# Seven half-size products in place of eight for the first expert layer, with a running sum in one PSUM bank

## The chip, the cores and the metric

One core of one Trainium2 chip. The metric is the time of one execution on the device in microseconds (us), as a median over repeated runs. All runs below were in the fast state, with a granted TensorE clock (as a share of full speed) of 0.98 or more over the span.

## The reference, cut to what matters

An attention over sorted blocks makes x (3072 tokens by 512), and a dense mixture of eight experts follows. The experts take four fifths of the time, and only their first layer is changed:

```python
N, D, E, F = (3072, 512, 8, 1024)
...
for e in range(E):
    h = np.maximum(x @ w1[e], 0.0)      # first layer: contraction over D = 512
    ye = h @ w2[e]                      # second layer: contraction over F = 1024
    out += P[:, e:e + 1] * ye
```

## The kernel before

The tokens stand in six columns of 512. One block of the first layer (`h_block`) makes 128 hidden features of one column with four matmuls of 128x512 in bf16, and ScalarE clamps it out of PSUM, the memory that matmuls write to and add up in. The kernel uses it as a ring of eight banks, each of which holds one result of 128x512; a bank can be used again when its result has been read out (evicted). One tile of the second layer (`y_tile`) takes eight matmuls, and VectorE scales it and adds it to the fp32 result. The first 76 blocks (experts 0 and 1) are made earlier, between the attention's matmuls. Then the expert loop runs: four tiles of one column, then the next blocks, up to nine columns ahead.

```python
    def bank(shape, dt=F32):                       # a ring of 8 PSUM banks
        return ps.tile(shape, dt, name="bank")
    # ... cut ...
    def h_block(e, c, fb, both=False):
        if fb == 0:
            hT[e, c] = hp_.tile([128, 8, 512], BF16, name="hTs")
        b_ = bank([128, 512])
        for kk in range(4):
            nc.tensor.matmul(b_, w1t[e][:, kk, fb * 128:(fb + 1) * 128], xf[:, kk, c * 512:(c + 1) * 512],
                             start=(kk == 0), stop=(kk == 3))
        # ... cut: while attention runs, every other one goes to VectorE ...
            nc.scalar.activation(out=hT[e, c][:, fb, :], in_=b_, func=AF.Relu)
    # ... cut ...
    def y_tile(e, c, tt):
        t = c * 4 + tt
        b_ = bank([128, Dm])
        for fb in range(8):
            nc.tensor.matmul(b_, hT[e, c][:, fb, tt * 128:(tt + 1) * 128], w2t[e][:, fb, :],
                             start=(fb == 0), stop=(fb == 7))
        # ... cut: expert 0 only scales ...
            nc.vector.scalar_tensor_tensor(out=osbl[:, t, :], in0=b_, scalar=glog[:, t, e:e + 1],
                                           in1=osbl[:, t, :], op0=ALU.mult, op1=ALU.add)
    # ... cut ...
    for n, (e, c) in enumerate(seq):               # 48 columns of experts
        for tt in range(4):
            y_tile(e, c, tt)
        # ... cut: weight loads ...
        while state["h"] < len(blocks) and (state["h"] // 8) - n < HB - 1:
            fill(1, both=False)                    # one h_block
```

The softmax here doesn't subtract the row's maximum and nothing guards it: scores larger than these inputs give would overflow.

Of the kernel before, what the change touches and what calls it, by code (L numbers as in the profile page):

```python
# [11 lines left out]

F32 = mybir.dt.float32
BF16 = mybir.dt.bfloat16
AF = mybir.ActivationFunctionType
AX = mybir.AxisListType
ALU = mybir.AluOpType
ENG = mybir.EngineType

def mkap(t, dims, off=0):  # L20
    return bass.AP(tensor=t.tensor, offset=t.offset + off, ap=dims)

@with_exitstack
def kernel(
# [11 lines left out]
    nc = tc.nc  # L36
    B, H, S, D = 4, 8, 768, 64
    NB = 8
    NPAIR = 16
    N, Dm, E, F = 3072, 512, 8, 1024  # L40
    NT = 24
    HB = 10
    scale = 1.0 / (D ** 0.5)

    ones = ctx.enter_context(tc.tile_pool(name="ones", bufs=1))
    wp = ctx.enter_context(tc.tile_pool(name="wp", bufs=2))
    hp_ = ctx.enter_context(tc.tile_pool(name="hp", bufs=HB))
    ps = ctx.enter_context(tc.tile_pool(name="ps", bufs=8, space=bass.MemoryType.PSUM))

    def bank(shape, dt=F32):  # L50
        return ps.tile(shape, dt, name="bank")
# [18 lines left out]
    kh = k.rearrange("b h (p kk) d -> (b h) p kk d", kk=6)  # L70
    vh = v.rearrange("b h (p kk) d -> (b h) p kk d", kk=6)
    actx = ExitStack()
    iop = actx.enter_context(tc.tile_pool(name="iop", bufs=5))
    atp_ = actx.enter_context(tc.tile_pool(name="atp", bufs=2))
    qkv = {}
# [9 lines left out]
    w1t, w2t = {}, {}  # L85

    def load_w1(e):
        w1t[e] = wp.tile([128, 4, F], BF16, name="w1e")
        nc.gpsimd.dma_start(out=w1t[e], in_=moe_w1[e].rearrange("(kk k) f -> k kk f", k=128))  # L89

    def load_w2(e):
        w2t[e] = wp.tile([128, 8, Dm], BF16, name="w2e")
        nc.gpsimd.dma_start(out=w2t[e], in_=moe_w2[e].rearrange("(fb k) f -> k fb f", k=128))  # L93
# [6 lines left out]
    xtT = ones.tile([128, 4, B, 6, 128], BF16)  # L100
    xf = xtT.rearrange("d hp b kk p -> d hp (b kk p)")
    glog = ones.tile([128, NT, E], F32)

    order = tc.manual_schedule(engines={ENG.PE, ENG.Activation, ENG.DVE, ENG.Pool, ENG.SP})
    order.__enter__()
# [3 lines left out]
        nc.tensor.matmul(w_, wide[:, 0:128], wide, start=True, stop=True)  # L109

    rs = ones.tile([32, 8], F32)
    Prep = ones.tile([32, 8, 8, 16], BF16)
    Pt = P.rearrange("p i j -> p j i")
    nc.vector.reduce_max(out=rs, in_=P, axis=AX.X)
    nc.vector.tensor_sub(P, P, mkap(rs, [rs.ap[0], rs.ap[1], [0, 8]]))
    for it in range(5):
# [4 lines left out]
                                op=ALU.mult)  # L121
        nc.vector.reduce_sum(out=rs, in_=Pt, axis=AX.X)  # L122
        nc.vector.reciprocal(out=rs, in_=rs)
        if it < 4:
            nc.vector.tensor_tensor(out=Pt, in0=Pt, in1=mkap(rs, [rs.ap[0], rs.ap[1], [0, 8]]),
                                    op=ALU.mult)
        else:
            nc.vector.tensor_tensor(out=Prep, in0=mkap(P, [P.ap[0], [8, 8], [1, 8], [0, 16]]),  # L128
                                    in1=mkap(rs, [rs.ap[0], [0, 8], [1, 8], [0, 16]]), op=ALU.mult)
    pbp = bank([128, 8, 32])  # L130
    for i in range(8):
        nc.tensor.matmul(pbp[:, i, :], Prep[:, i].rearrange("g j c -> g (j c)"),
                         ident[0:32, 0:32], start=True, stop=True)
    Pbig = ones.tile([128, 8, 32], F32)
    nc.vector.tensor_copy(Pbig, pbp)

    KT, VT, QT, ATT, VS, OG = {}, {}, {}, {}, {}, {}

    vs_ = [ones.tile([96, 8, 2, 65], BF16, name=f"vs{n}") for n in range(2)]
    for t in vs_:  # L140
        nc.vector.memset(t[:, :, :, 64:65], 1.0)

# [87 lines left out]

    hT = {}
    flip = [0]

    def h_block(e, c, fb, both=False):
        if fb == 0:
            hT[e, c] = hp_.tile([128, 8, 512], BF16, name="hTs")
        b_ = bank([128, 512])
        for kk in range(4):
            nc.tensor.matmul(b_, w1t[e][:, kk, fb * 128:(fb + 1) * 128], xf[:, kk, c * 512:(c + 1) * 512],  # L239
                             start=(kk == 0), stop=(kk == 3))  # L240
        flip[0] ^= 1
        if both and flip[0]:
            nc.vector.tensor_scalar_max(hT[e, c][:, fb, :], b_, 0.0)  # L243
        else:
            nc.scalar.activation(out=hT[e, c][:, fb, :], in_=b_, func=AF.Relu)  # L245

    early = [(0, 0), (1, 0), (0, 1), (0, 2), (1, 1), (1, 2), (0, 3), (1, 3), (0, 4), (0, 5), (1, 4), (1, 5)]
    seq = early + [(e, c) for e in range(2, E) for c in range(6)]
    blocks = [(e, c, fb) for e, c in seq for fb in range(8)]
    last_batch = [0, 1, 1, 2, 3, 3]  # L250
    state = {"h": 0, "done": -1}

    def spin(n):
        b_ = bank([128, 512])
        for _ in range(n):
            nc.tensor.matmul(b_, wide[:, 0:128], wide, start=True, stop=True)  # L256

    def fill(n, both=True):
        for _ in range(n):
            if state["h"] >= len(blocks):  # L260
                return
            e, c, fb = blocks[state["h"]]
            if last_batch[c] > state["done"]:
                if state["done"] < 0:
                    spin(1)
                return
            h_block(e, c, fb, both)
            state["h"] += 1
# [33 lines left out]
    for it in range(8):  # L302
# [3 lines left out]
                                op=ALU.mult)  # L306
        nc.vector.reduce_sum(out=cs2, in_=glog.rearrange("p t e -> p e t"), axis=AX.X)
        fill(3, both=False)
        b_ = bank([128, E])
# [3 lines left out]
                                       in1=mkap(cs1, [cs1.ap[0], [0, NT], cs1.ap[1]]),  # L313
                                       op0=ALU.mult, op1=ALU.mult)
# [4 lines left out]
    osbl = mpc.tile([128, NT, Dm], F32)  # L319
# [3 lines left out]
# [6 lines that stand above are left out]
        if e == 0:  # L329
            nc.vector.tensor_scalar(out=osbl[:, t, :], in0=b_, scalar1=glog[:, t, e:e + 1],  # L330
                                    scalar2=None, op0=ALU.mult)
        else:
            nc.vector.scalar_tensor_tensor(out=osbl[:, t, :], in0=b_, scalar=glog[:, t, e:e + 1],  # L333
                                           in1=osbl[:, t, :], op0=ALU.mult, op1=ALU.add)
        if e == E - 1:
            bb, kk = divmod(t, 6)
            nc.sync.dma_start(out=out[bb * S:(bb + 1) * S].rearrange("(p kk) d -> kk p d", kk=6)[kk],
                              in_=osbl[:, t, :])

    left = {e: 6 for e in range(E)}  # L340
    hleft = {e: 6 for e in range(E)}
    for e, c, fb in blocks[:state["h"]]:
        if fb == 7:
            hleft[e] -= 1
    if hleft[0] == 0:
        load_w1(2)
    if hleft[1] == 0:
        load_w1(3)
    for n, (e, c) in enumerate(seq):
        for tt in range(4):  # L350
            y_tile(e, c, tt)
        left[e] -= 1
        if left[e] == 0 and e + 2 < E:
            load_w2(e + 2)
        while state["h"] < len(blocks) and (state["h"] // 8) - n < HB - 1:
            e1, _, fb1 = blocks[state["h"]]
            fill(1, both=False)
            if fb1 == 7:
                hleft[e1] -= 1
                if hleft[e1] == 0 and e1 + 2 < E:  # L360
                    load_w1(e1 + 2)
    order.__exit__(None, None, None)

_INS = ['q', 'k', 'v', 'sort_net', 'moe_w_gate', 'moe_w1', 'moe_w2']
# [25 lines left out]
```

## Time and profile before

| | before |
|---|---|
| time, median of 13 runs | 749.34 us (748.73 to 750.14) |
| span of the profiled execution | 748.3 us |
| TensorE busy | 98% |
| ScalarE / VectorE / GpSimd busy | 37% / 34% / 7% |

Matmuls overlap, so the TensorE row of "busy" says little about stalls; the distance from start to start does.

### The profile page before, as it was taken

How to read it: one execution, taken by the hardware profiler on the slowest of the kernel's cores; microseconds unless marked ns; L12 is line 12 of the kernel's file. 1: busy time of each engine (PE TensorE's matmuls, PEld its weight loads, DVE VectorE, ACT ScalarE, POOL GpSimd, SP SyncE). 2: the span in 40 equal slices, each digit the busy share in tenths (PEclk: the TensorE clock that was granted, in tenths of full speed). 3: DMA queues.
4: the chain of work that ended last, by engine and by line, in shares of the span. 5: the costliest groups of instructions: out<-in, count | busy, mean ns of one | idle time of the engine just before them, and what ended most of it. 6: DMA issues, size and time to landing. Idle time of an engine off the chain costs nothing.

```text
span 748.3 us, 10583 instructions
## 1 busy us (share of the span) xinstructions
PE 733.7 (98%) x4508; PEld 358.5 (48%) x4588; DVE 252.1 (34%) x497; ACT 274.2 (37%) x497; POOL 48.9 (7%) x71
## 2 busy tenths in 40 slices
PE   6999999999999999999999999999999999999997
PEld 3776665444444444444444444444444444444443
DVE  5887775632122122121221221221221221212443
ACT  2776665513423423324324324234234233243000
POOL 7542000000000000000000000000000000000000
PEclk8999999999999999999999999999999999999999
DMA  9999100011300062200330032100330003000133
GB/s 147 204 205 165 19 2 1 1 22 36 56 1 1 0 95 31 44 1 1 56 57 1 0 57 40 18 0 1 57 56 1 1 0 57 1 0 1 43 154 141
DMA packets 29679, 33.21 MB, mean 44 GB/s; under 512 B 1984, under 2 KB 22464, under 8 KB 29632
## 3 DMA queue, kind: packets, MB, share of 16 engines
q0 software_dynamic: 26128, 26.23, 22.4%
q1 hardware_dynamic: 3504, 6.30, 2.2%
q8 instruction: 36, 0.59, 0.3%
q14 instruction: 11, 0.09, 0.0%
HBM read 52.45 MB, written 6.29 MB: 79 GB/s over the span
## 4 chain that ended last, share of the span: by engine, by line
PE 97%; DVE 1%; issue 1%; ACT 0%; DMA 0%; ACTq 0%
PE bank L327 44%; PE bank L239 44%; PE bank L162 2%; PE bank L207 2%; PE bank L195 1%; PE bank L188 1%; PE bank L256 1%; PE bank L218 1%; PE bank L173 1%; PE bank L227 0%; DMA P<-in_sort_net_dram 0%; PE bank L310 0%; DVE rs L122 0%; ACT P L117 0%; DVE Prep L128 0%
## 5 line engine op out<-in xcount | busy, mean ns | idle before, releaser
L245 ACT ACTIVATE hTs<-bank 128x512 bf16<-128x512 f32 x358 | 213.7, 597 | 371.2 <-PE bank L239 363.1
L239 PE MATMUL bank<-xtT,w1e 128*128 128x512 bf16 x1490 | 341.9, 379 | 1.9
L327 PE MATMUL bank<-w2e,hTs 128*128 128x512 bf16 x1503 | 336.0, 379 | 1.7
L333 DVE SCALAR_TENSOR_TENSOR osbl<-bank,glog,osbl 128x512 f32<-128x512 f32 x168 | 126.1, 751 | 398.8 <-PE bank L327 386.0
L327 PEld LDWEIGHTS <-hTs 128*128 128x128 bf16 x1536 | 150.3, 98 | 181.0
L239 PEld LDWEIGHTS <-w1e 128*128 128x128 bf16 x1536 | 147.8, 98 | 170.3
L330 DVE TENSOR_SCALAR osbl<-bank,glog 128x512 f32<-128x512 f32 x24 | 18.0, 751 | 54.7 <-PE bank L327 51.7
L191 ACT ACTIVATE at<-bank 96x384 bf16<-96x384 f32 x64 | 26.0, 486 | 8.7 <-PE bank L188 8.4
L211 DVE TENSOR_TENSOR OG<-bank,rc 96x256 bf16<-96x256 f32 x64 | 26.9, 421 | 2.2
L89 POOL DMA_DIRECT2D w1e<-in_moe_w_dram x8 | 6.0, 754 | 312.6 <-PE bank L239 312.3
L93 POOL DMA_DIRECT2D w2e<-in_moe_w_dram x8 | 7.1, 890 | 237.5 <-PE bank L327 161.9
L243 DVE TENSOR_SCALAR hTs<-bank 128x512 bf16<-128x512 f32 x26 | 17.8, 683 | 6.1 <-PE bank L239 6.1
L220 ACT COPY xtT<-bank 128x768 bf16<-128x768 bf16 x16 | 12.8, 799 | 14.1 <-PE bank L218 13.7
L167 ACT CAST KT<-bank 128x384 bf16<-128x384 f32 x32 | 13.8, 485 | 8.1 <-PE bank L162 7.9
L207 PEld LDWEIGHTS <-at 96*96 96x96 bf16 x256 | 14.1, 125 | 2.8
L207 PE MATMUL bank<-vs,at 96*96 96x65 bf16 x256 | 13.9, 209 | 0.0
L81 POOL DMA_DIRECT2D kb<-in_k_dram x16 | 11.5, 718 | 18.5 <-PE bank L162 16.8
L169 DVE CAST VT<-bank 128x384 bf16<-128x384 f32 x16 | 8.9, 553 | 11.2 <-PE bank L162 8.8
L198 DVE COPY vs<-bank 96x1024 bf16<-96x1024 bf16 x16 | 11.0, 690 | 4.2 <-PE bank L195 3.8
L210 DVE RECIPROCAL rc<-bank 96x4 f32<-96x4 f32 x64 | 10.9, 170 | 3.7 <-PE bank L207 3.7
L81 POOL DMA_DIRECT2D vb<-in_v_dram x16 | 11.5, 717 | 7.4 <-PE bank L162 2.8
L81 POOL DMA_DIRECT2D qb<-in_q_dram x16 | 11.5, 717 | 2.1 <-PE bank L256 0.9
(57 smaller groups left out, 187.2 us busy)
## 6 DMA issues: line engine op xcount, KB each, us to landing
w1e<-in_moe_w_dram POOLq DMA_DIRECT2D x8, 1024.0 KB, 8.0
w2e<-in_moe_w_dram POOLq DMA_DIRECT2D x8, 1024.0 KB, 8.8
out_dram<-osbl SPq DMA_DIRECT2D x24, 256.0 KB, 2.0
kb<-in_k_dram POOLq DMA_DIRECT2D x16, 192.0 KB, 8.2
vb<-in_v_dram POOLq DMA_DIRECT2D x16, 192.0 KB, 7.5
qb<-in_q_dram POOLq DMA_DIRECT2D x16, 192.0 KB, 7.6
P<-in_sort_net_dram SPq DMA_DIRECT2D x1, 8.0 KB, 1.6
wg<-in_moe_w_gate_dram POOLq DMA_DIRECT2D x1, 8.0 KB, 6.7
```

The source lines that it names most:

```text
L81: nc.gpsimd.dma_start(out=t, in_=src[2 * m:2 * m + 2].rearrange("h p kk d -> p h kk d"))
L162: nc.tensor.matmul(b_[64 * h2:64 * h2 + 64, k3, :], src[:, h2, 3 * kh2 + k3, :], R[:, h2].rearrange("p i c -> p (i c)"), start=True, stop= ...
L167: nc.scalar.copy(dst, b_)
L191: nc.scalar.activation(out=ATT[m][h2][:, half, :], in_=bb[h2].rearrange("k i q -> k (i q)"), func=AF.Exp, scale=scale)
L207: nc.tensor.matmul(b_[:, i4, :], ATT[m][h2][:, half, 96 * i4:96 * i4 + 96], VS[m][:, i, h2, :], start=True, stop=True)
L211: nc.vector.tensor_tensor(out=OG[m][:, 4 * half:4 * half + 4, h2, :], in0=b_[:, :, 0:64], in1=mkap(rc, [rc.ap[0], [1, 4], [0, 64]]), op=AL ...
L239: nc.tensor.matmul(b_, w1t[e][:, kk, fb * 128:(fb + 1) * 128], xf[:, kk, c * 512:(c + 1) * 512], start=(kk == 0), stop=(kk == 3))
L243: nc.vector.tensor_scalar_max(hT[e, c][:, fb, :], b_, 0.0)
L245: nc.scalar.activation(out=hT[e, c][:, fb, :], in_=b_, func=AF.Relu)
L327: nc.tensor.matmul(b_, hT[e, c][:, fb, tt * 128:(tt + 1) * 128], w2t[e][:, fb, :], start=(fb == 0), stop=(fb == 7))
L330: nc.vector.tensor_scalar(out=osbl[:, t, :], in0=b_, scalar1=glog[:, t, e:e + 1], scalar2=None, op0=ALU.mult)
L333: nc.vector.scalar_tensor_tensor(out=osbl[:, t, :], in0=b_, scalar=glog[:, t, e:e + 1], in1=osbl[:, t, :], op0=ALU.mult, op1=ALU.add)
```

## The change

The intent is to do less multiplying. Take a 2x2 block product: two halves of the 1024 hidden features, two halves of the contraction, two token columns. The plain way needs eight half-size products. A scheme of Strassen's kind (Winograd's form) needs seven, at the price of four sums of weight blocks, four sums of token blocks, and sums of the products. The change does this for experts 2 to 7:

- VectorE makes the token sums once; GpSimd makes the weight sums for each expert.
- Four of the products are added up in one PSUM bank (`al`). ScalarE copies the running sum out after each of the first three, and clamps it out after the fourth. VectorE adds copies and other banks, and clamps (`relu_add`).
- The steps of one group stand between pieces of four second-layer matmuls.
- The hidden buffers, sums and copies are carved from one large tile, and prefetch falls from nine columns to three.

```diff
-    HB = 10
+    HB = 12
-    hp_ = ctx.enter_context(tc.tile_pool(name="hp", bufs=HB))
+    big = ones.tile([128, HB, 4096], BF16)         # cut: carve(), h_slot(): views of it
+    def x_sums(c):                                 # 3 column pairs, on VectorE
+        nc.vector.tensor_sub(T1, B12, B11)
+        nc.vector.tensor_sub(T2, B22, T1)
+        nc.vector.tensor_sub(T3, B22, B12)
+        nc.vector.tensor_sub(T4, B21, T2)
+    def w_sums(e):                                 # on GpSimd: S1 to S4, alike
+        nc.gpsimd.tensor_tensor(out=S1, in0=A21, in1=A22, op=ALU.add)
+        ...
+    def relu_add(out, a, b):                       # max(min(a + b, s0), 0)
+        nc.vector._custom_dve(TENSOR_ADD_SAT, out=out, in0=a, in1=b, s0=3.4028234663852886e38, s1=0.0)
+    def dq(e, c, j):                               # prod(): two matmuls
+        al = bank([128, 512])
+        prod(al, A11, B11, True)
+        nc.scalar.copy(cP1, al)
+        be = bank([128, 512])
+        prod(be, A12, B21, True)
+        relu_add(h0[:, j, :], be, cP1)
+        yield
+        prod(al, S2, T2, False)                    # adds to al
+        nc.scalar.copy(cU2, al)
+        ga = bank([128, 512])
+        prod(ga, S1, T1, True)
+        nc.scalar.copy(cP5, ga)
+        yield
+        prod(al, S3, T3, False)
+        nc.scalar.copy(cU3, al)
+        prod(ga, S4, B22, False)
+        relu_add(h1[:, j, :], ga, cU2)
+        relu_add(h1[:, 4 + j, :], cU3, cP5)
+        yield
+        prod(al, A22, T4, False)
+        nc.scalar.activation(out=h0[:, 4 + j, :], in_=al, func=AF.Relu)
+        yield
     for n, (e, c) in enumerate(seq):
         for tt in range(4):
-            y_tile(e, c, tt)
+            for part in range(2):
+                y_half(e, c, tt, part)             # four matmuls of a tile
+                if state["h"] < len(blocks):
+                    fill(1, both=False)            # the 20 blocks left of expert 0 and 1
+                elif n >= 9:
+                    l1_step()                      # dq up to its next yield
+        if n == 7:                                 # cut: the sums of experts 4 to 7, loads
+            for cc in range(3):
+                x_sums(cc)
+            w_sums(2)
+            w_sums(3)
```

More of the change, by code (lines that the diff above doesn't have):

```diff
@@ L11 @@
 from concourse._compat import with_exitstack
+from concourse.dve_ops import TENSOR_ADD_SAT
 F32 = mybir.dt.float32
@@ L41 @@
     NT = 24
-    HB = 10
+    HB = 12
+    KB = 1024
     scale = 1.0 / (D ** 0.5)
@@ L72 @@
     actx = ExitStack()
+    onca = actx.enter_context(tc.tile_pool(name="onca", bufs=1))
     iop = actx.enter_context(tc.tile_pool(name="iop", bufs=5))
@@ L102, with carve @@
     glog = ones.tile([128, NT, E], F32)
+    big = ones.tile([128, HB, 4096], BF16)
+    bigf = big.rearrange("p s n -> p (s n)")
+    def carve(shape, dt, off):
+        n = 1
+        for d_ in shape[1:]:
+            n *= d_
+        n = n * (2 if dt == F32 else 1)
+        v_ = bigf[:, off // 2:off // 2 + n]
+        if dt == F32:
+            v_ = v_.bitcast(F32)
+        names = "abcd"[:len(shape) - 1]
+        return v_.rearrange("p (" + " ".join(names) + ") -> p " + " ".join(names),
+                            **{k_: d_ for k_, d_ in zip(names, shape[1:])})
     order = tc.manual_schedule(engines={ENG.PE, ENG.Activation, ENG.DVE, ENG.Pool, ENG.SP})
@@ L111 @@
     rs = ones.tile([32, 8], F32)
-    Prep = ones.tile([32, 8, 8, 16], BF16)
+    Prep = onca.tile([32, 8, 8, 16], BF16)
     Pt = P.rearrange("p i j -> p j i")
@@ L133 @@
                          ident[0:32, 0:32], start=True, stop=True)
-    Pbig = ones.tile([128, 8, 32], F32)
+    Pbig = onca.tile([128, 8, 32], F32)
     nc.vector.tensor_copy(Pbig, pbp)
     KT, VT, QT, ATT, VS, OG = {}, {}, {}, {}, {}, {}
-    vs_ = [ones.tile([96, 8, 2, 65], BF16, name=f"vs{n}") for n in range(2)]
+    vs_ = [onca.tile([96, 8, 2, 65], BF16, name=f"vs{n}") for n in range(2)]
     for t in vs_:
@@ L232, with h_slot @@
     flip = [0]
+    made = [0]
+    def h_slot():
+        n = made[0]
+        made[0] += 1
+        slot = n if n < HB else HB - 5 + (n - HB) % 5
+        return carve([128, 8, 512], BF16, 8 * KB * slot)
     def h_block(e, c, fb, both=False):
         if fb == 0:
-            hT[e, c] = hp_.tile([128, 8, 512], BF16, name="hTs")
+            hT[e, c] = h_slot()
         b_ = bank([128, 512])
@@ L248 @@
     seq = early + [(e, c) for e in range(2, E) for c in range(6)]
-    blocks = [(e, c, fb) for e, c in seq for fb in range(8)]
+    blocks = [(e, c, fb) for e, c in early for fb in range(8)]
     last_batch = [0, 1, 1, 2, 3, 3]
@@ L338, in y_tile @@
                               in_=osbl[:, t, :])
-    left = {e: 6 for e in range(E)}
-    hleft = {e: 6 for e in range(E)}
-    for e, c, fb in blocks[:state["h"]]:
-        if fb == 7:
-            hleft[e] -= 1
-    if hleft[0] == 0:
-        load_w1(2)
-    if hleft[1] == 0:
-        load_w1(3)
+    xS = [carve([128, 2, 3, 512], BF16, 6 * KB * n) for n in range(4)]
+    wS = [[carve([128, 2, 512], BF16, (24 + 8 * s + 2 * n) * KB) for n in range(4)]
+          for s in range(2)]
+    cps = [[carve([128, 512], F32, (40 + 8 * s + 2 * n) * KB) for n in range(4)]
+           for s in range(2)]
@@ new lines @@
+    xv = xf.rearrange("d kk (c h t) -> d kk c h t", h=2, t=512)
+    def x_sums(c):
+        B11, B12, B21, B22 = (xv[:, 2 * kh:2 * kh + 2, c, h, :] for kh in range(2) for h in range(2))
+        T1, T2, T3, T4 = (t[:, :, c, :] for t in xS)
+        nc.vector.tensor_sub(T1, B12, B11)
[3 more added lines that the diff above has]
+    def w_sums(e):
+        w = w1t[e]
+        A11, A12, A21, A22 = (w[:, 2 * kh:2 * kh + 2, 512 * fh:512 * fh + 512] for fh in range(2) for kh in range(2))
+        S1, S2, S3, S4 = wS[e % 2]
+        nc.gpsimd.tensor_tensor(out=S1, in0=A21, in1=A22, op=ALU.add)
+        nc.gpsimd.tensor_tensor(out=S2, in0=S1, in1=A11, op=ALU.subtract)
+        nc.gpsimd.tensor_tensor(out=S3, in0=A11, in1=A21, op=ALU.subtract)
+        nc.gpsimd.tensor_tensor(out=S4, in0=A12, in1=S2, op=ALU.subtract)
@@ new lines, in relu_add, with prod @@
+    def relu_add(out, a, b):
+        nc.vector._custom_dve(TENSOR_ADD_SAT, out=out, in0=a, in1=b, s0=3.4028234663852886e38, s1=0.0)
+    ndq = [0]
+    def dq(e, c, j):
+        if j == 0:
+            hT[e, 2 * c] = h_slot()
+            hT[e, 2 * c + 1] = h_slot()
+        h0, h1 = hT[e, 2 * c], hT[e, 2 * c + 1]
+        w = w1t[e]
+        A11 = w[:, 0:2, 0:512]
+        A12 = w[:, 2:4, 0:512]
+        A22 = w[:, 2:4, 512:1024]
+        S1, S2, S3, S4 = wS[e % 2]
+        B11 = xv[:, 0:2, c, 0, :]
+        B21 = xv[:, 2:4, c, 0, :]
+        B22 = xv[:, 2:4, c, 1, :]
+        T1, T2, T3, T4 = (t[:, :, c, :] for t in xS)
+        cP1, cP5, cU2, cU3 = cps[ndq[0] % 2]
+        ndq[0] += 1
+        def prod(b_, A, Bm, first):
+            for kk in range(2):
+                nc.tensor.matmul(b_, A[:, kk, 128 * j:128 * j + 128], Bm[:, kk, :],
+                                 start=(first and kk == 0), stop=(kk == 1), skip_group_check=True)
+        al = bank([128, 512])
[20 more added lines that the diff above has]
+        yield
@@ new lines, in y_half @@
+    def y_half(e, c, tt, part):
+        t = c * 4 + tt
+        if part == 0:
+            ybank[0] = bank([128, Dm])
+        b_ = ybank[0]
+        for fb in range(4 * part, 4 * part + 4):
+            nc.tensor.matmul(b_, hT[e, c][:, fb, tt * 128:(tt + 1) * 128], w2t[e][:, fb, :],
+                             start=(fb == 0), stop=(fb == 7))
+        if part == 0:
+            return
+        if e == 0:
+            nc.vector.tensor_scalar(out=osbl[:, t, :], in0=b_, scalar1=glog[:, t, e:e + 1],
+                                    scalar2=None, op0=ALU.mult)
+        else:
+            nc.vector.scalar_tensor_tensor(out=osbl[:, t, :], in0=b_, scalar=glog[:, t, e:e + 1],
+                                           in1=osbl[:, t, :], op0=ALU.mult, op1=ALU.add)
+        if e == E - 1:
+            bb, kk = divmod(t, 6)
+            nc.sync.dma_start(out=out[bb * S:(bb + 1) * S].rearrange("(p kk) d -> kk p d", kk=6)[kk],
+                              in_=osbl[:, t, :])
@@ new lines, with l1_step @@
+    ybank = [None]
+    load_w1(2)
+    load_w1(3)
+    late = seq[12:]
+    l1 = []
+    for e, c in late:
+        if c % 2 == 0:
+            for j in range(4):
+                l1.append((e, c // 2, j))
+    pos = [0]
+    cur = [None]
+    def l1_step():
+        if cur[0] is None:
+            if pos[0] >= len(l1):
+                return
+            e, c, j = l1[pos[0]]
+            cur[0] = dq(e, c, j)
+        try:
+            next(cur[0])
+        except StopIteration:
+            cur[0] = None
+            e, c, j = l1[pos[0]]
+            pos[0] += 1
+            if c == 2 and j == 3 and e + 2 < E:
+                load_w1(e + 2)
+            if c == 0 and j == 3 and e >= 3 and e + 1 < E:
+                w_sums(e + 1)
+            l1_step()
@@ L349 @@
     for n, (e, c) in enumerate(seq):
         for tt in range(4):
-            y_tile(e, c, tt)
-        left[e] -= 1
-        if left[e] == 0 and e + 2 < E:
-            load_w2(e + 2)
-        while state["h"] < len(blocks) and (state["h"] // 8) - n < HB - 1:
-            e1, _, fb1 = blocks[state["h"]]
-            fill(1, both=False)
-            if fb1 == 7:
-                hleft[e1] -= 1
-                if hleft[e1] == 0 and e1 + 2 < E:
-                    load_w1(e1 + 2)
+            for part in range(2):
[3 more added lines that the diff above has]
+                elif n >= 9:
+                    l1_step()
@@ L362 @@
+        if n == 7:
[3 more added lines that the diff above has]
+            w_sums(3)
+        if c == 5 and e + 2 < E:
+            load_w2(e + 2)
     order.__exit__(None, None, None)
```

## The prediction

> **What bounds the kernel now.** I read the page first: which engine is busy, and whether evenly.
>
> ```profile
> span 748.3 us, 10583 instructions
> PE 733.7 (98%) x4508; PEld 358.5 (48%) x4588; DVE 252.1 (34%) x497; ACT 274.2 (37%) x497; POOL 48.9 (7%) x71
> PE   6999999999999999999999999999999999999997
> ...
> PEclk8999999999999999999999999999999999999999
> ...
> PE 97%; DVE 1%; issue 1%; ACT 0%; DMA 0%; ACTq 0%
> ```
>
> TensorE is at nine tenths or more in every slice but the first and last, at full clock, and 97% of the chain that ended last is TensorE. A busy TensorE can still be a stalling one, because the page models matmul ends, so next I took the rate from the longest pieces of the chain and from a timeline of one stretch:
>
> ```profile
> 474.82 6.91 PE bank L239 x32
> ...
> 495.54 6.91 PE bank L327 x32
> ```
>
> ```profile
> 322.71 7.07 PE L239 MATMUL bank<-xtT,w1e 128*128 128x512 bf16 x32
> ...
> 323.83 0.60 ACT L245 ACTIVATE hTs<-bank 128x512 bf16<-128x512 f32 x1 [7.23 <-PE bank L239]
> 324.64 0.60 ACT L245 ACTIVATE hTs<-bank 128x512 bf16<-128x512 f32 x1 [0.21 <-PE bank L239]
> 325.50 0.60 ACT L245 ACTIVATE hTs<-bank 128x512 bf16<-128x512 f32 x1 [0.27 <-PE bank L239]
> ```
>
> 32 matmuls of 128x512 take 6.91 us from start to start, 215.9 ns each (one alone is shown as 379 ns, so each overlaps the next by 163 ns; 31 x 0.2159 + 0.379 = 7.07 agrees). The expert loop starts on TensorE at 146.59 us in the timeline. It holds 48 x 32 = 1536 second-layer matmuls and (384 - 76) x 4 = 1232 first-layer ones (76 of the 384 first-layer blocks are done before it), 2768 in all. 2768 x 0.2159 = 597.6 us; 146.6 + 597.6 = 744.2 us, and the last matmul of the trace ends at 744.18 us. So the loop has no stall at all: its time is a count of matmuls times 215.9 ns. After it come 4.1 us for the last eviction and the last output transfer. The other engines wait for TensorE:
>
> ```profile
> L245 ACT ACTIVATE hTs<-bank 128x512 bf16<-128x512 f32 x358 | 213.7, 597 | 371.2 <-PE bank L239 363.1
> ...
> L333 DVE SCALAR_TENSOR_TENSOR osbl<-bank,glog,osbl 128x512 f32<-128x512 f32 x168 | 126.1, 751 | 398.8 <-PE bank L327 386.0
> ```
>
> ScalarE's idle time of 371 us and VectorE's 399 us ahead of these groups are nearly all waits for matmuls. There is room for side work.
>
> **What the Trainium skill says.** "TensorE: Matmul & The Clock Gate", section "Wait — 56ns, not 53.3ns?": warm matmuls start N / 2.4 GHz plus about 2.5 ns apart, 215.7 ns at N = 512. The trace agrees (215.9). "VectorE: DVE Perf Modes", section "The perf-mode tier table": a tensor_tensor of bf16 in SBUF runs at two elements a cycle, an fp32 one or one with PSUM at one. The trace has no such bf16 tensor_tensor; its 96x1024 bf16 copies took 690 ns and its 32x1024 tensor_tensor from fp32 1212 ns, which I take as the two cases. "GPSIMD Engine Reference", section "3.1 Elementwise — side-by-side cycle accounting": a GpSimd tensor_tensor of 2048 fp32 elements took 4497 ns; half of that, 2.2 us, is my estimate for 1024. No GpSimd arithmetic of that size is in the trace. "PSUM — Partial Sum Buffer", section "The four PSUM rules": a synchronised read of a partial sum within an accumulation group is allowed; the change rests on this for its results, and nothing in this trace shows it.
>
> **The change part by part.**
>
> *Removed.* For experts 2 to 7 the first layer becomes a seven-product scheme of Strassen's kind. A 2x2 block product (two halves of the 1024 hidden features, two halves of the contraction, two 512-token columns) takes seven products in place of eight. One step group now makes four 128x512 blocks with 7 x 2 = 14 matmuls in place of 4 x 4 = 16. There are 6 experts x 3 column pairs x 4 = 72 groups, so 72 x 2 = 144 matmuls go; the instruction order of TensorE confirms it (8866 rows against 9154: 144 matmuls and 144 weight loads). Each is on the path: 144 x 0.2159 = 31.1 us. The loop falls to 2624 x 0.2159 = 566.5 us.
>
> *Moved.* Order and waits up to the loop are the same instruction by instruction. The loop is now interleaved: four second-layer matmuls, then two or four first-layer ones. Prefetch falls from nine columns to three, which only matters if a consumer comes early: a column pair is finished in 16 half-tiles and used one column after that, so it doesn't. The hidden buffers are carved from one tile; the waits in the built program name the exact earlier readers, so I expect no false dependence.
>
> *Added per group, beside TensorE.* One group with its four half-tiles of second-layer work is 14 + 16 = 30 matmuls, 6.48 us. ScalarE does four copies and one relu, 5 x 0.597 = 3.0 us (46%). VectorE does three new add-and-clamp operations and two evictions; I put the custom ones at the 0.751 us of L333, 5 x 0.75 = 3.75 us (58%). Both fit.
>
> *Added on the path, perhaps.* One PSUM bank collects four products and is copied out between them, so TensorE must wait for the copy before it adds the next. In matmul slots of 0.2159 us, the products on that bank stand at slots 0-1, 8-9, 16-17 and 24-25, and those on a second bank at 10-11 and 18-19. First wait: slot 1 ends at 0.22 + 0.38 = 0.60, the copy runs from 0.65 (the timeline shows ScalarE start 0.04 to 0.09 us after the last matmul) to 1.25, slot 8 is due at 1.73: 0.4 us to spare after some 0.1 us for the signal back. The tightest is the second bank: ScalarE copies slot 9's result from 2.36 to 2.96, then slot 11's (which ended at 2.75) to about 3.6, and slot 18 is due at 3.89. With the signal back some 0.2 us remain. So 0 stall in steady state; I allow 0.01 us x 72 = about 0.7 us for the odd late one.
>
> *Added once.* Twelve VectorE sums of 128x1024 bf16 stand after column 7's evictions, and hold up those of column 8. Column 8 starts at 146.59 + 336 x 0.2159 = 219.1 us. The sums run from 0.9 us after that for 12 x (0.69 + 0.05) = 8.9 us, to 9.8; the first eviction of column 8 then ends at 10.6. TensorE needs that bank as its ninth (four for column 8; one second-layer bank and three of the group's own; then this one), at 32 + 16 = 48 slots, 10.4 us. Stall 0.3 us. GpSimd's eight weight sums wait for the slots of columns 3 and 4 (read until 191.5 and 198.4 us) and end by about 210 us at 2.2 us each; they are needed at about 228 us. Later ones have tens of us.
>
> Sum: 749.4 - 31.1 + 0.7 + 0.3 = 719.3 us.
>
> **The rivals.**
>
> *The copy becomes the wait.* If a fp32-writing copy takes longer than the relu's 597 ns, or the signal back more than 0.2 us, TensorE stalls once in each group. 0.1 us x 72 gives 7 us (726); 0.3 us gives 22 us (740, the gain nearly gone). For it: the margin is only 0.2 us, and the bank is reused in place. Against it: fp32 evictions in the gate follow the same size law as bf16 ones (211 ns for 48 elements, 485 for 384), so the output type costs nothing.
>
> *VectorE becomes the bound.* If a custom add-and-clamp took 1.7 us, VectorE would need 3 x 1.7 + 2 x 0.75 = 6.6 us a group, over 6.48: hardly a loss of 1% (about 725), more if GpSimd's sums block it. Nothing in the trace shows the custom operation; against it stands that its bytes are those of L333.
>
> *The sums run at one element a cycle.* Twelve at 1.22 us end at 15.9 us, and TensorE stands for some 6 us: 725, or a little more if the clock falls with it. Or GpSimd's sums take over 4.5 us each: then the first group waits for its weights by a few us.
>
> *Nothing gained.* That needs TensorE not to have been the bound; the count of matmuls that meets the last one's end to 0.1 us speaks against it.
>
> **Range and chances.** The floor is 749.4 - 31.1 = 718.3 us less run-to-run spread (748.7 to 750.1), so 717.0 below. Above, one rival in its mild form gives 725 to 726. A gain of under 2% (over 734.4 us) needs a stall of 0.22 us in every group, or two rivals at once: 0.05. Slower by 2% needs over 46 us of stalls: 0.01.
>
> **What would show it.** Right: first-layer matmuls of the group line and the old line together 144 fewer; 32 matmuls in any steady stretch still 6.91 us apart; TensorE over 99% busy in the loop; no wait of TensorE for ScalarE in the table of waits; one gap under 1 us near 230 us; ScalarE copies of 597 ns; last matmul near 713.5 us. Wrong: TensorE waits for the copies or sums with a total of several us, custom operations over 1 us, or VectorE busy near 100% in the loop. The prediction fails if those stalls sum to more than 7 us.

## The result, and the profile after

The changed kernel took 718.55 us (median of 8 runs, 717.65 to 718.81), the kernel before 749.34 us. The ratio is 0.9588 (95% interval 0.9578 to 0.9597). Ratios here are the mean time of one kernel's fast runs over that of the other's fast runs of the same rounds, so not quite the ratio of the medians quoted. 719.3 us was predicted.

The page of the changed kernel (span, busy times, TensorE and its clock in 40 slices, chain):

```profile
span 716.7 us, 10909 instructions
...
PE 701.5 (98%) x4367; PEld 343.7 (48%) x4444; DVE 394.7 (55%) x725; ACT 307.1 (43%) x569; POOL 101.3 (14%) x95
PE   6999999999999999999999999999999999999997
PEclk8999999999999999999999999999999999999999
...
PE 97%; DVE 1%; issue 1%; DMA 0%; ACT 0%
```

Weight loads (PEld) fell from 4588 to 4444, by 144, as the count said. (Some matmul records are missing from a trace, so count the loads.) VectorE went from 34% to 55%, GpSimd from 7% to 14%, and the chain is still 97% TensorE.

The groups of instructions of the changed kernel, by form (busy us, mean ns of one, idle before and its releaser):

```profile
L416 ACT COPY big<-bank 128x512 f32<-128x512 f32 x72 | 42.2, 586 | 95.1 <-PE bank L411 95.1
L388 DVE CUSTOM_DVE_ANT_0 big<-bank,big 128x512 bf16<-128x512 f32 x144 | 99.6, 692 | 219.2 <-PE bank L411 137.5 <-ACT big L416 81.7
L388 DVE CUSTOM_DVE_ANT_0 big<-big 128x512 bf16<-128x512 f32 x72 | 49.5, 688 | 0.0
...
L382 POOL TENSOR_TENSOR big<-w1e 128x1024 bf16<-128x1024 bf16 x6 | 12.7, 2121 | 37.3 <-DMA w1e<-in_moe_w_dram 29.1 <-PE bank L443 8.2
```

None of these operations was in the trace before. A copy into fp32 took 586 ns (597 assumed), the custom add-and-clamp 692 and 688 ns (751 assumed), a weight sum 2.12 us (2.2 assumed).

One group in the timeline of the changed kernel (start, length, engine, line):

```profile
232.76 1.03 PE L411 MATMUL bank<-xtT,w1e 128*128 128x512 bf16 x4
233.40 0.59 ACT L416 COPY big<-bank 128x512 f32<-128x512 f32 x1 [0.64 <-PE bank L411]
...
234.49 1.03 PE L411 MATMUL bank<-big 128*128 128x512 bf16 x4
...
235.12 0.59 ACT L422 COPY big<-bank 128x512 f32<-128x512 f32 x1 [1.14 <-PE bank L411]
...
235.60 0.59 ACT L425 COPY big<-bank 128x512 f32<-128x512 f32 x1
...
236.22 0.59 PE L411 MATMUL bank<-big 128*128 128x512 bf16 x2
236.65 0.59 PE L411 MATMUL bank<-xtT,big 128*128 128x512 bf16 x2
...
239.24 1.03 PE L411 MATMUL bank<-xtT,w1e 128*128 128x512 bf16 x4
```

From one group's first product to the next is 239.24 - 232.76 = 6.48 us, 30 matmuls of 0.216 us: no stall. The loop as a whole says the same: in this trace it runs from 146.00 us (first second-layer matmul) to 712.51 us (end of the last), 566.5 us, which is the prediction's 2624 x 0.2159, against 597.6 us before. It is 31.1 us shorter; the start-up before it differs by 0.6 us between the two profiles. The first copy ends at 233.99 us and the product that must wait for it starts at 234.49, 0.5 us later. The copy of the second bank (L425) ends at 236.19 and its product starts at 236.65. It had begun at 235.60, 0.11 us before the copy ahead of it ended. I had put them end to end and so counted too small a margin there. The Trainium skill's page "ScalarE: Activation LUTs", section "What ACT_TABLE_LOAD costs", says that ACTIVATE instructions overlap by about 93 ns back to back; I had not used it. The copies of this trace overlap by about as much, 0.11 us.

The waits of TensorE in the changed kernel, complete:

```profile
PE bank L148 <- DVE Prep L144: 4.5, 1, 4.5
PE bank L125 <- DVE wide L62: 1.2, 1, 1.2
PE bank L178 <- DVE R L163: 1.0, 1, 1.0
PE bank L279 <- PE bank L189: 0.3, 1, 0.3
```

These lines belong to the start-up and the attention; there is none of the expert loop. (The table leaves out very short waits, as e4 will show; the count of the loop leaves no room for them here.) At the point where the token sums hold VectorE, the timeline shows:

```profile
219.39 0.68 DVE L373 TENSOR_TENSOR big<-xtT 128x1024 bf16<-128x1024 bf16 x1
...
226.38 0.69 DVE L376 TENSOR_TENSOR big<-xtT,big 128x1024 bf16<-128x1024 bf16 x1
...
226.99 2.72 DVE L448 TENSOR_SCALAR osbl<-bank,glog 128x512 f32<-128x512 f32 x4
...
228.88 1.03 PE L443 MATMUL bank<-w2e,big 128*128 128x512 bf16 x4
```

The twelve sums take 219.39 to 227.07, so they start 0.64 us apart though each is shown as 0.68 us or more. The first held-up eviction ends near 227.7, and the matmul that needs its bank starts at 228.88. That is 1.1 us to spare, where a stall of 0.3 us was predicted.

### The profile page after: what moved, and what is told of

It reads as the page before. It is cut to its first block, busy times and chain, and to the rows that moved or that the text cites.

```text
span 716.7 us, 10909 instructions
## 1 busy us (share of the span) xinstructions
PE 701.5 (98%) x4367; PEld 343.7 (48%) x4444; DVE 394.7 (55%) x725; ACT 307.1 (43%) x569; POOL 101.3 (14%) x95
## 4 chain that ended last, share of the span: by engine, by line
PE 97%; DVE 1%; issue 1%; DMA 0%; ACT 0%
PE bank L443 46%; PE bank L411 31%; PE bank L262 11%; PE bank L178 2%; PE bank L223 2%; PE bank L211 1%; PE bank L204 1%; PE bank L279 1%; PE bank L234 1%; PE bank L189 1%; PE bank L243 0%; DMA P<-in_sort_net_dram 0%; PE bank L333 0%; DVE rs L138 0%; ACT P L133 0%
## 5 line engine op out<-in xcount | busy, mean ns | idle before, releaser
L443 PE MATMUL bank<-w2e,big 128*128 128x512 bf16 x1499 | 377.4, 379 | 1.2
L443 PEld LDWEIGHTS <-big 128*128 128x128 bf16 x1536 | 150.3, 98 | 181.0
L388 DVE CUSTOM_DVE_ANT_0 big<-bank,big 128x512 bf16<-128x512 f32 x144 | 99.6, 692 | 219.2 <-PE bank L411 137.5
L411 PE MATMUL bank<-big 128*128 128x512 bf16 x418 | 113.7, 379 | 0.8
L262 PE MATMUL bank<-xtT,w1e 128*128 128x512 bf16 x359 | 91.3, 379 | 0.8
L411 PEld LDWEIGHTS <-big 128*128 128x128 bf16 x576 | 56.4, 98 | 68.0
L416 ACT COPY big<-bank 128x512 f32<-128x512 f32 x72 | 42.2, 586 | 95.1 <-PE bank L411 95.1
L422 ACT COPY big<-bank 128x512 f32<-128x512 f32 x72 | 42.2, 586 | 82.1 <-PE bank L411 82.1
L434 ACT ACTIVATE big<-bank 128x512 bf16<-128x512 f32 x72 | 43.0, 597 | 78.1 <-PE bank L411 78.1
L411 PE MATMUL bank<-xtT,w1e 128*128 128x512 bf16 x288 | 73.9, 379 | 0.0
L411 PEld LDWEIGHTS <-w1e 128*128 128x128 bf16 x432 | 42.3, 98 | 51.0
L428 ACT COPY big<-bank 128x512 f32<-128x512 f32 x72 | 42.2, 586 | 51.1 <-PE bank L411 50.5
L268 ACT ACTIVATE big<-bank 128x512 bf16<-128x512 f32 x70 | 41.8, 597 | 35.4 <-PE bank L262 33.5
L262 PEld LDWEIGHTS <-w1e 128*128 128x128 bf16 x384 | 35.1, 100 | 34.5
L388 DVE CUSTOM_DVE_ANT_0 big<-big 128x512 bf16<-128x512 f32 x72 | 49.5, 688 | 0.0
L411 PE MATMUL bank<-xtT,big 128*128 128x512 bf16 x144 | 42.8, 379 | 0.7
L425 ACT COPY big<-bank 128x512 f32<-128x512 f32 x72 | 42.6, 591 | 0.0
```

The source lines that it names most:

```text
L388: nc.vector._custom_dve(TENSOR_ADD_SAT, out=out, in0=a, in1=b, s0=3.4028234663852886e38, s1=0.0)
L411: nc.tensor.matmul(b_, A[:, kk, 128 * j:128 * j + 128], Bm[:, kk, :], start=(first and kk == 0), stop=(kk == 1), skip_group_check=True)
L416: nc.scalar.copy(cP1, al)
L422: nc.scalar.copy(cU2, al)
L425: nc.scalar.copy(cP5, ga)
L428: nc.scalar.copy(cU3, al)
```

## The experiments

Each kernel below is the changed kernel with one edit, and all gave correct results. The diffs are cut to the lines that matter. Times are to be set against 718.55 us.

### e1_eight_products: the arithmetic undone, all else kept

```diff
-            cur[0] = dq(e, c, j)
+            cur[0] = dq8(e, c, j)    # four h_blocks of 4 matmuls + relu, one per step
```

> The changed kernel with one thing undone: each group makes its four blocks with 4 x 4 = 16 matmuls and four relu evictions on ScalarE, in four steps of 4, between the same second-layer matmuls. Buffers, interleaving, loads and (now unused) sums stay. Theory 1 (the gain is the count of matmuls alone): 144 more matmuls at 0.2159 us give 718.5 + 31.1 = 749.6 us, the time before. Rival (part of the gain came from the new interleaving, buffers or loads): clearly under 749 us.

Measured: 749.24 us (748.75 to 750.22, 12 runs), beside 749.69 us for the kernel before; ratio 0.9999 (0.9990 to 1.0008). The interleaving, the shorter prefetch, the large tile and 36 sums that run for nothing together change nothing to within 0.1%. So the whole gain comes with the form of the product.

### e2_half_experts: half of the dose

```diff
-            cur[0] = dq(e, c, j)
+            cur[0] = (dq8 if e < 5 else dq)(e, c, j)
```

> As the first run, but only for experts 2, 3 and 4; experts 5, 6 and 7 keep the seven products. Theory 1 (a count): 72 of the 144 matmuls come back, 718.5 + 15.5 = 734.1 us. Rival (a once-only gain or cost at the change between the two forms, or a gain that depends on where in the loop it stands): off that line by more than 1 us.

Measured: 734.30 us (733.89 to 734.51); ratio to the kernel before 0.9794 (0.9779 to 0.9808), clearly faster, though whether by 2% the interval leaves open. 0, 72 and 144 matmuls removed give 749.24, 734.30 and 718.55 us: 14.9 and 15.8 us for 72 matmuls each, 0.208 and 0.219 us per matmul around the 0.2159 of the timeline. The gain is a count.

### e3_no_interleave: the steps of a group together

```diff
-                elif n >= 9:
-                    l1_step()
+                elif n >= 9 and (tt % 2, part) == (0, 0):
+                    for _ in range(4):
+                        l1_step()
```

> The four steps of a group are issued without second-layer matmuls between them; those follow in one piece. Same instructions otherwise. Theory 1 (the running sum in one bank has a chain of copies that is hidden only by the second-layer matmuls between): with a copy of 0.586 us, 0.04 us to its start and an estimated 0.1 us for the signal back, the waits in a group are about 0.48, 0.48, 0.16 and 0.31 us, 1.4 us in all; 72 x 1.4 = 103 us, so about 820 us, slower than before the change. Rival (TensorE has other work to pull forward, or the copies overlap the next matmuls): within 5 us of 718.5.

Measured: 809.34 us (808.77 to 809.80), 8% slower than the kernel before the change. The same 144 matmuls are saved; now the copies are waited for. One of three like waits of TensorE in this run (us in total, times, longest), and its timeline:

```profile
PE bank L411 <- ACT big L428: 17.4, 72, 0.5
```

```profile
404.47 1.03 PE L411 MATMUL bank<-xtT,w1e 128*128 128x512 bf16 x4
405.10 0.58 ACT L416 COPY big<-bank 128x512 f32<-128x512 f32 x1 [3.29 <-PE bank L411]
...
405.74 1.02 PE L411 MATMUL bank<-big 128*128 128x512 bf16 x4 [0.24 <-ACT big L416]
...
408.32 0.59 PE L411 MATMUL bank<-big,w1e 128*128 128x512 bf16 x2 [0.24 <-ACT big L428]
...
408.75 2.54 PE L443 MATMUL bank<-w2e,big 128*128 128x512 bf16 x11
```

The table's idle of 0.24 us a wait understates the loss, because it counts from the modelled end of the matmul before. Start to start tells it: the group's 14 matmuls would take 14 x 0.216 = 3.02 us and take 408.75 - 404.47 = 4.28 us. 1.26 us x 72 = 90.7 us, and 718.55 + 90.7 = 809.2: the measured time. I had said 1.4 us a group. The signal back to TensorE takes 405.74 - 405.68 = 0.06 us and not 0.1, and the second bank's copy overlaps the first's, so that each of the first bank's three waits is 0.40 us from start to start and the second bank's 0.06.

### e4_gap_of_two: two second-layer matmuls between the steps, not four

```diff
-        for fb in range(4 * part, 4 * part + 4):
+        for fb in range(2 * part, 2 * part + 2):
...
-            for part in range(2):                  # and the last part is 1
+            for part in range(4):                  # and the last part is 3
...
-                elif n >= 9:
+                elif n >= 9 and tt % 2 == 0:
                     l1_step()
```

> Two second-layer matmuls between the steps of a group in place of four; the other eight follow the group. Theory 1, with the same sums: waits of about 0.03, 0.02 and 0.16 us in a group (the last for the second bank's copy, which queues behind the first's on ScalarE), 72 x 0.2 = 15 us, about 733 us; if the signal back takes 0.05 us and not 0.1, about 0.1 us a group and 726. Rival (there is a lot of room): 718.5 us.

Measured: 720.04 us (719.61 to 721.18), 1.5 us more than the change, 0.02 us a group. The timeline of this run shows why it is so little:

```profile
401.16 0.58 ACT L416 COPY big<-bank 128x512 f32<-128x512 f32 x1 [1.99 <-PE bank L411]
...
401.39 0.60 PE L443 MATMUL bank<-w2e,big 128*128 128x512 bf16 x2
...
401.83 1.03 PE L411 MATMUL bank<-big 128*128 128x512 bf16 x4
...
402.94 0.59 ACT L425 COPY big<-bank 128x512 f32<-128x512 f32 x1
403.12 0.60 PE L411 MATMUL bank<-big 128*128 128x512 bf16 x2
403.58 0.59 PE L411 MATMUL bank<-xtT,big 128*128 128x512 bf16 x2
```

The first bank's copy ends at 401.74 and its product, due at 401.39 + 0.43 = 401.82, starts on time but for the rounding. The second bank's copy (L425) ends at 403.53 and its product, due at 403.12 + 0.43 = 403.55, starts at 403.58: 0.03 us late, and the groups of this trace are 6.50 us apart against 6.48. A gap of two is the edge. The 733 us were wrong, and so was the 726 for a faster signal: both counted 0.1 us or more for the second bank, whose wait is 0.03 us, as its copy starts early. With e3, the loss per group is 1.26, 0.02 and 0 us for gaps of zero, two and four matmuls. Each wait is the part of a copy that the matmuls in front of it do not cover, and two of them cover nearly all of it; no run has a gap of one.

### e5_sums_twice: a longer burst on VectorE

```diff
-            for cc in range(3):
-                x_sums(cc)
+            for cc in range(6):
+                x_sums(cc % 3)
```

> The twelve sums of token columns on VectorE are made twice, same values. In the changed kernel they start every 0.633 us and end at 227.07 us of the span, and the matmul that needs the first bank freed after them starts at 228.88 us. Theory 1 (a burst on VectorE is free only as long as the eight banks last): 12 x 0.633 = 7.6 us more, the first eviction then ends at 235.4 us, TensorE stands for about 6.6 us, 725 us, or a little more if its clock falls in the gap. Rival (banks or evictions give more room than I count): 718.5 us.

Measured: 726.90 us (726.31 to 727.25), 8.4 us more. One of TensorE's waits in this run, and three stretches of 8 us (busy us and instructions of PE, weight loads, VectorE, ScalarE, GpSimd; then the granted clock, the DMA share and GB/s):

```profile
PE bank L443 <- DVE osbl L448: 5.8, 1, 5.8
```

```profile
220.00:228.00 8.00, 7.64 (x37) 3.28 (x36) 7.90 (x14) 0.59 (x1) 0.00 (x0) 1.00 0.00 0
228.00:236.00 8.00, 2.18 (x7) 0.79 (x8) 7.93 (x13) 1.07 (x2) 0.00 (x0) 0.81 0.00 0
236.00:244.00 8.00, 8.00 (x30) 3.27 (x29) 5.49 (x9) 2.27 (x5) 0.00 (x0) 0.77 0.00 0
```

The banks run out as counted, and the wait of 5.8 us has a second price: the granted clock is 0.81 and 0.77 over the two stretches after it begins. From 234.84 to 240.27 us TensorE started 14 matmuls in 5.43 us where 3.02 would do, 2.4 us lost. One distance between two groups in this trace is 15.39 us in place of 6.48, all others are as before. So 8.9 us went in this one place: 2.4 to the slow matmuls, 6.0 from start to start to the wait for the bank, and 0.5 to a wait that the edit itself made (a product waits for a token sum that is written a second time). The Trainium skill's page "TensorE: Matmul & The Clock Gate", section "What's actually happening", has half the clock after an idle window of some 3.4 us; the matmuls that started 0.43 us apart for 5 us here agree with half. So by my estimate the rival of the prediction in which the sums run at half speed would have cost about 8 us: the 6 us of standing, and 2.4 us for what it left as "a little more if the clock falls with it".

### e6_clamp_twice and e7_clamp_thrice: where VectorE becomes the bound

```diff
-        nc.vector._custom_dve(TENSOR_ADD_SAT, ...)
+        for _ in range(2):           # range(3) in e7
+            nc.vector._custom_dve(TENSOR_ADD_SAT, ...)
```

> Each add-and-clamp on VectorE is done twice, same values. VectorE then needs 6 x 0.69 + 2 x 0.75 = 5.6 us of the 6.48 us of a group with its second-layer matmuls. Theory 1 (work beside the bound is free while it fits and no bank waits for it): 718.5 us, within 1.5. Rival (the banks are held longer by it and TensorE waits): several us more.

> Each add-and-clamp three times. VectorE needs 9 x 0.69 + 2 x 0.75 = 7.7 us a group, over the 6.48 us that TensorE needs, and becomes the bound. Theory 1: 72 x (7.7 - 6.48) = 88 us more, about 805 us (a few us less for the slack of the banks). Rival: VectorE's operations overlap each other enough to stay near 6.5 us a group: under 730 us.

Measured: 718.82 us twice (718.07 to 719.03), no change, with VectorE at 76% of the span; 795.04 us thrice (two runs, 794.42 and 795.66), 76.5 us more. In the thrice run, whose lines are numbered one higher, TensorE has this wait:

```profile
PE bank L444 <- DVE big L389: 55.8, 63, 1.5
```

TensorE now waits for banks that VectorE has not yet read. In this timeline a group takes 7.47 us (its first products start at 401.95 and 409.42), against 7.7 predicted, because VectorE's instructions overlap: from the start of a triple of clamps to the next instruction is 2.05 us, 0.68 us for each clamp, and from an eviction to the next 0.66 us, though each is shown as 0.69 to 0.74; 3 x 2.05 + 2 x 0.66 = 7.47. (The repeats of one clamp start 0.72 us apart, but the instruction behind them 0.61 us after the last. In the changed kernel one clamp follows another after 0.61 us too, so a repeat costs VectorE somewhat more than one more real addition would.)

Of the 71 distances between groups in this trace 55 are 7.47 us, ten are shorter (6.47 to 6.90) and six longer (8.14 to 11.84, together 13.9 us more than 6 x 7.47); they sum to 75.6 us more than in the changed kernel, which is nearly the whole loss. In the six stand eight clamps that took 1.36 to 2.65 us, together 10.5 us over the usual 0.69. All eight have two inputs in SBUF and ran while a weight sum of GpSimd did; none of the 432 clamps with a PSUM input took over 0.72 us. One of the eight is the last of this triple:

```profile
408.11 4.03 DVE L389 CUSTOM_DVE_ANT_0 big<-big 128x512 bf16<-128x512 f32 x3
```

This triple reads two tiles of SBUF and met a weight sum of GpSimd (409.47 to 411.59 us). It took 4.03 us; the like one of the group before, from 400.64 us, took 2.13. In the changed kernel itself four such additions took 0.72 to 0.86 us, and a weight sum up to 2.57 us where none took over 2.12 in e1, which has no such additions; there it costs nothing. Nor did it in e6, where eight clamps were slowed, to at most 2.50 us.

### e8_copy_twice: where the copies become the wait

```diff
-        nc.scalar.copy(cP1, al)
+        nc.scalar.copy(cP1, al)
+        nc.scalar.copy(cP1, al)      # and so for cU2, cP5, cU3
```

> Each of the four copies on ScalarE is done twice in a row, same values; ScalarE still has 8 x 0.586 + 0.597 = 5.3 us of work in a group of 6.48 us. Theory 1 (the length of the copies is on the path as soon as it passes the gap of four second-layer matmuls): waits of about 0.18, 0.18 and 0.74 us, the last for the second bank, whose copies queue behind the first's; 72 x 1.1 = 79 us, about 797 us. Rival (only ScalarE's total matters, and it fits): 718.5 us.

Measured: 789.04 us (two runs, 788.88 and 789.21), 70.5 us more, 0.98 us a group against 1.1 predicted. ScalarE is at 60% of the span. TensorE's wait and the timeline of this run (L447 is the second layer here):

```profile
PE bank L411 <- ACT big L428: 37.0, 72, 0.5
```

```profile
407.49 1.03 PE L447 MATMUL bank<-w2e,big 128*128 128x512 bf16 x4
...
408.51 0.59 PE L411 MATMUL bank<-big 128*128 128x512 bf16 x2
...
409.62 0.59 PE L411 MATMUL bank<-xtT,big 128*128 128x512 bf16 x2 [0.51 <-ACT big L428]
```

L428 here is the second copy of the second bank. Its product is due 0.43 us after 408.51, at 408.94, and starts at 409.62: 0.68 us late (0.74 predicted). The one ahead was due at 407.49 + 0.86 = 408.35 and is 0.16 us late (0.18 predicted). So the copies' length, not ScalarE's total, is what TensorE waits for, and four matmuls of gap do not cover a copy made twice. (The repeat of a copy starts 0.62 us after it, without overlap; copies of different banks, back to back, start 0.48 us apart.)

## Why the prediction was right

- *TensorE is the bound and the time is a count of matmuls.* Right. e1 gives the saving back to within 0.1% (its interval), and e2 takes half of it back; 31.1 us were predicted, 749.34 - 718.55 = 30.8 us measured, and the loop in the traces is 31.1 us shorter.
- *Order, buffers and prefetch cost nothing.* Right: e1 has them all, at ratio 0.9999.
- *VectorE and ScalarE fit beside it.* Right, with smaller numbers than assumed (586 and 692 ns against 597 and 751). e6 and e7 show how much room VectorE has: twice the additions are free, three times are not.
- *The copies are hidden, the tightest with 0.2 us.* Right in kind. The term was mis-sized: the tightest margin is near 0.4 us, since the second bank's copy starts 0.11 us before the first's ends, where the prediction put them end to end, and the signal back takes 0.06 us, not 0.1. The same term made the forecasts for e3, e4 and e8 too high. That the interleaving carries the change is shown by e3: without it, seven products are 8% slower than eight.
- *The burst of sums stalls TensorE by 0.3 us.* Wrong by the sign of a small term. The sums start 0.64 us apart, not 0.74, so 1.1 us were to spare. This and the 0.7 us allowed for late copies are 1.0 us of stall that did not come; the forecast lay 0.75 us high.
- *The rivals.* The copy as the wait, VectorE as the bound and the slow burst were each made real (e8, e7, e5) and cost 70.5, 76.5 and 8.4 us. None holds in the change itself, nor does the one of slow weight sums: they took 2.1 to 2.6 us, not 4.5.
- *Slips in the sums.* VectorE at 6.6 us a group would add 72 x 0.12 = 8.6 us, which makes about 727 us and not 725. Twelve sums at 1.22 us, with the 0.05 us between them that the prediction allows elsewhere, end at 16.1 us and not 15.9. By its own terms the last matmul belonged near 146.6 + 566.5 + 1.0 = 714.1 us, not 713.5; it ended at 712.51. None of them enters the 719.3.

Not settled: whether the second layer could take seven products too, which no run tries. It has as many matmuls as the first; if its sums fell on VectorE, e6 and e7 say that the room there ends between two and three times the present additions.

## What to carry to other kernels

Where TensorE starts its matmuls back to back, better overlap has nothing left to give. Fewer matmuls helped here, and each removed one was worth its start-to-start distance, not the duration that the trace shows. A scheme that trades matmuls for additions pays as long as each engine beside it fits, and as long as every copy that a later matmul must wait for has other matmuls in front of it: here two of 128x512 between the steps were the edge and four were safe. Count the gap for each wait, for the loss without one (1.26 us a group here) is about three times the saving (0.43 us a group).

## What the Trainium skill lacked or had wrong

- "VectorE: DVE Perf Modes" has no figure for a custom add-and-clamp: 128x512, fp32 in and bf16 out, took 692 ns with one PSUM input and 688 ns with both in SBUF. (Its section on the TRN2 errata has 691 ns for an fp32 tensor_tensor add of 512 elements, and the custom operation came within 3 ns of it; the 751 ns assumed came from another operation of the trace.)
- "ScalarE: Activation LUTs" does not say when back-to-back instructions overlap: copies of different banks overlapped by 0.11 us, but in e8 a copy repeated from the same bank into the same tile started 0.62 us after the first, 0.03 us after its end.
- "GPSIMD Engine Reference", section "3.1 Elementwise — side-by-side cycle accounting", has fp32 alone: a bf16 tensor_tensor of 128x1024 took 2.12 us.
- "SBUF — State Buffer", section "Who interferes with whom", names the contention of VectorE instructions that have two SBUF inputs with GpSimd's reads, which e7 agrees with, but gives no size for a pair like this one: three such additions took 4.03 us in place of 2.13, and in the changed kernel a GpSimd sum took up to 2.57 us in place of 2.12.
- "PSUM — Partial Sum Buffer", section "The four PSUM rules", allows a read in the middle of an accumulation group without saying what it costs: copy of 128x512 to fp32 586 ns (the relu of a finished bank takes 597), start of the copy 0.04 us after the matmul's end, and 0.06 us from the copy's end to the next matmul.
- No page that I read has an estimate for a scheme with seven products: here 144 fewer matmuls in the loop gave 30.8 us. The outputs are right.
